# Sliding-window attention and a SwiGLU block: the first gate and value products begun with the head pairs that are ready, and q, k and v of later batches loaded earlier

## The chip, the core and the metric

One core of a Trainium2 chip runs the whole program. The time is device microseconds for one execution. Three runs of the kernel before took 276.92, 277.04 and 277.45 us.

## The reference

Attention over 4 batches, 8 heads, 768 positions and 64 columns per head, with 8 global keys and a window of 96, then a feed-forward block on the 3072 tokens of 512 columns.

```python
scores = scale * np.matmul(q, k.transpose(0, 1, 3, 2))
keep = is_global | is_local
bias = -slopes[:, None, None] * dist[None, :, :]
a = softmax(np.where(keep, scores + bias, -1e9))     # cut
x = (a @ v).transpose(0, 2, 1, 3).reshape(3072, 512)
g = x @ w_gate
silu = g * (1.0 / (1.0 + np.exp(-g)))
out = (silu * (x @ w_val)) @ w_out
```

## The kernel before, in words

The heads of a batch go in four pairs. A pair has four kinds of steps: `transposes` (q and k are turned on TensorE into `trq` and `trk`, and copied to `qT` and `kT`), `scores` (three banks `bk` 0 to 2 of key chunks; exp on ScalarE into `at`, then a product with the masks on VectorE or POOL, L234 and L238), and `values` for either half of the 768 queries (`den` and `num` on TensorE, two VectorE transposes and a reciprocal, and the product that writes `xT`; on VectorE in batch 0, L282, and on POOL later, L279). `xT` holds the attention's output with the columns of a head pair on the partitions, so that pair `hp` is contraction chunk `c = hp` of the products that follow.

The feed-forward block runs over 8 blocks `t` of 384 tokens. Each block has 12 groups `f` of 128 columns; for each, `gate_or_val` makes a gate product (`gps`) and a value product (`vps`) of four matmuls, one per chunk `c`, in one PSUM bank each. ScalarE makes `th` from the gate, VectorE `sl` from `th` and the gate (L313) and `hT` from `sl` and the value (L317). `out_part` (`ops`) turns `hT` of block `t - 1` into output rows, three matmuls at a time. The banks of the products go round by `state["x"]`: `x0`, `x1`, `x2`, `o0` in block 0 and the first three later, so that the third gate waits until VectorE has read the first.

Order is written out by hand, and each engine takes its instructions in that order. The prologue (L378 to L386) runs the four pairs of batch 0 for the first half, two stages apart. Then the list `groups` (gates, values, output parts) is walked, and the steps of the attention still to do (`plan`) are put between them: each group has a work number, a quota turns work into steps, and when a whole step is owed it is issued.

All loads are DMAs that POOL issues in its own queue, between its products; a DMA converts float32 to float16. Those of batch 0, the weights, and parts of batch 1 stand ahead of everything else (L342 to L362). The rest is issued at fixed places: `loads` (L424 to L431) maps 12 `t` + `f` to `load_qk` and `load_v_rest`. An issue waits until the load eight places ahead of it in the queue has landed.

Of the kernel before, what the change touches and what calls it, by code (L numbers as in the profile page):

```python
# [9 lines left out]
FP32 = mybir.dt.float32  # L10
# [27 lines left out]
def kernel(  # L38
# [18 lines left out]
    NP = H // 2  # L57
# [4 lines left out]
    NC = DM // 128  # L62
    J = S // 128
    NCH = 7
    TB = 384
# [18 lines left out]
    ps = ctx.enter_context(tc.tile_pool(name="ps", bufs=1, space=bass.MemoryType.PSUM))  # L84
# [21 lines left out]
    def stage(b):  # L106
        qst[b] = sb2.tile([128, H, J * D], FP16, name="qst", tag="qst")
        kst[b] = sb2.tile([128, H, J * D], FP16, name="kst", tag="kst")

    def load_qk(b, h0, h1):  # L110
        for st, src in ((qst[b], q), (kst[b], k)):
            nc.gpsimd.dma_start(  # L112
                out=st[:, h0:h1, :],
                in_=src[b, h0:h1].rearrange("h (p j) d -> p h (j d)", p=128))
# [6 lines left out]
    def load_v_rest(b, c):  # L121
        n = min(KC, S - KC * c)
        nc.gpsimd.dma_start(  # L123
            out=vSs[b][NG:NG + n, c, :, :],
            in_=v[b, :, KC * c:KC * c + n, :].rearrange("h p d -> p h d"))
# [18 lines left out]
    def load_w(g):  # L144
        f0 = WF * g
        for w, src in ((wg, moe_w_gate), (wv, moe_w_val)):
            nc.gpsimd.dma_start(
                out=w[:, :, f0:f0 + WF],
                in_=src[:, f0:f0 + WF].rearrange("(c p) f -> p c f", p=128))

    def load_wo(g):
        nc.gpsimd.dma_start(
            out=wo[:, 4 * g:4 * g + 4, :],
            in_=moe_w_out[512 * g:512 * g + 512].rearrange("(f p) d -> p f d", p=128))
# [4 lines left out]
    attn_tags = ["a0", "a1", "a2", "a3"]  # L159
    pro_tags = ["a0", "a1", "a2", "a3", "x0", "x1", "x2", "o0"]  # L160
    state = {"tags": pro_tags, "n": 0, "x": ["x0", "x1", "x2", "o0"]}
# [8 lines left out]
    def make_masks(h, c0, c1):  # L170
        nc.scalar.activation(
            out=masks[:, h, c0:c1], in_=dist[:, c0:c1], func=AF.Exp, scale=-slopes[h])
# [3 lines left out]
    def run_later(n):  # L176
        for _ in range(n):
            if later:
                later.pop(0)()
# [114 lines left out]

    gv = {}

    def gate_or_val(t, f, which):
        if f == 0 and which == 0:
            hTs[t] = sb2.tile([128, NFF, TB], FP16, name="hT", tag="hT")
        w = (wg, wv)[which]  # L300
        dst = ps.tile([128, 512], FP32, name="gv"[which] + "ps", tag=state["x"][gv.get("n", 0) % len(state["x"])])
        gv["n"] = gv.get("n", 0) + 1
        for c in range(NC):
            nc.tensor.matmul(  # L304
                dst[:, 0:TB], lhsT=w[:, c, 128 * f:128 * f + 128],
                rhs=xT[:, c, TB * t:TB * t + TB],
                start=(c == 0), stop=(c == NC - 1))

        if which == 0:
            th = sb2.tile([128, TB], FP32, name="th", tag="th")  # L310
            nc.scalar.activation(out=th, in_=dst[:, 0:TB], func=AF.Tanh, scale=0.5)  # L311
            sl = sb2.tile([128, TB], FP32, name="sl", tag="sl")
            nc.vector.scalar_tensor_tensor(  # L313
                out=sl, in0=th, scalar=1.0, in1=dst[:, 0:TB], op0=AluOp.add, op1=AluOp.mult)
            gv["sl"] = sl
        else:
            nc.vector.tensor_mul(hTs[t][:, f, :], dst[:, 0:TB], gv["sl"])  # L317
# [3 lines left out]
    def out_part(t, i, part):  # L321
        if part == 0:
            tag = ["a0", "a1", "o0"][i] if t == TOK // TB - 1 else "o0"
            ops_t[0] = ps.tile([128, 512], FP32, name="ops", tag=tag)
        ops = ops_t[0]
        for f in range(3 * part, 3 * part + 3):
            nc.tensor.matmul(  # L327
                ops, lhsT=hTs[t][:, f, 128 * i:128 * i + 128], rhs=wo[:, f, :],
                start=(f == 0), stop=(f == NFF - 1))
        if part == 3:  # L330
            osb = sb2.tile([128, DM], FP32, name="osb", tag="osb")
            nc.scalar.mul(out=osb, in_=ops, mul=0.5)  # L332
            r0 = TB * t + 128 * i
            nc.sync.dma_start(out=out[r0:r0 + 128, :], in_=osb)
# [17 lines left out]
    for c in range(4, NCH):  # L352
        load_v_rest(0, c)
    load_w(2)
    load_w(3)
    load_wo(0)
    load_qk(1, 0, 2)
    load_wo(1)
    load_wo(2)
    load_qk(1, 2, 4)  # L360
# [6 lines left out]
    def early(hp, s):  # L367
        p = pairs[0, hp]
        if s == 0:
            p.transposes()  # L370
        elif s < 3:
            p.scores(s - 1, nc.vector)
        else:
            p.values(0, True)

    make_masks(0, 0, BANK)
    make_masks(1, 0, BANK)
    for t in range(4 + 2 * (NP - 1)):  # L378
        for hp in range(NP):
            s = t - 2 * hp  # L380
            if 0 <= s < 4:
                early(hp, s)
                run_later(9)
                if s == 1 and hp + 1 < NP:
                    make_masks(2 * hp + 2, 0, BANK)
                    make_masks(2 * hp + 3, 0, BANK)  # L386
    for h in range(H):
        make_masks(h, BANK, 3 * WIN)
    state["tags"] = attn_tags
    state["n"] = 0  # L390


    def sc(b, hp, bk):
# [29 lines left out]

    loads = {10: [lambda: load_qk(1, 4, 8)]}  # L424
    for c in range(4, NCH):
        loads[14 + c] = [lambda c=c: load_v_rest(1, c)]
    for b, base, step in ((2, 23, 1), (3, 38, 2)):
        loads[base] = [lambda b=b: (stage(b), load_qk(b, 0, 4))]
        loads[base + step] = [lambda b=b: load_qk(b, 4, 8)]
        for c in range(NCH):  # L430
            loads[base + step * (2 + c)] = [lambda b=b, c=c: load_v_rest(b, c)]  # L431
# [3 lines left out]
    groups = []  # L435
    for t in range(NT):
        for f in range(NFF):
            groups.append((t, f, 1.0, lambda t=t, f=f: gate_or_val(t, f, 0)))
            groups.append((t, f, 1.0, lambda t=t, f=f: gate_or_val(t, f, 1)))
            if t > 0:  # L440
                groups.append((t, f, 1.1, lambda t=t, f=f: out_part(t - 1, f // 4, f % 4)))
    todo, quota = [], {}
# [67 lines left out]
```

## Time and profile before

| | |
|---|---|
| median of three runs | 277.04 us |
| the profiled execution | 276.11 us |
| its span, first to last instruction | 274.3 us |
| TensorE (PE) busy | 250.5 us, 91% |
| VectorE (DVE) busy | 179.6 us, 65% |
| ScalarE (ACT) busy | 141.4 us, 52% |
| POOL busy | 113.4 us, 41% |
| mean granted TensorE clock | 0.988 |

Times in the rows are microseconds from the start of the span. A row of the timeline gives the start, the duration, the engine, the line, what is written and read, how many instructions it joins and, in brackets, how long the engine stood idle ahead and who released it. A matmul's duration is from its start to its modelled end, so that matmuls in a row overlap. A granted clock of 1.00 is 2.4 GHz and 0.50 is 1.2 GHz. "PEld" is the loading of a matmul's weights.

### The profile page before, as it was taken

What the parts mean: (1) busy time and instruction counts of PE and PEld (TensorE: products, weight loads), DVE (VectorE), ACT (ScalarE), POOL (GpSimd) and SP (SyncE); (2) the same over time, 40 slices, a digit from 0 to 9 for tenths busy, and PEclk for the clock granted to TensorE, in tenths of its full rate; (3) what the DMA queues carried; (4) which work ended last, traced back from release to release, by engine and by line L of the source; (5) the groups of instructions that cost most, each with busy time, mean ns of one, the idle gap of its engine ahead of it and who ended that gap; (6) DMA issues with size and microseconds to landing.
All of it is one profiled execution on the core that took longest, in us unless ns stands there. A gap on an engine that the chain in (4) does not pass through costs nothing.

```text
span 274.3 us, 5703 instructions
## 1 busy us (share of the span) xinstructions
PE 250.5 (91%) x2240; PEld 143.3 (52%) x2240; DVE 179.6 (65%) x389; ACT 141.4 (52%) x297; POOL 113.4 (41%) x130
## 2 busy tenths in 40 slices
PE   1786988899999599998999999999999999999994
PEld 0563355555556364655556555565556555555541
DVE  2588697878778539576674778576787855555520
ACT  3678445486656365766456646665473333323321
POOL 8965535164358906741756517344171400000000
PEclk9998699999999999999999999999999999999999
DMA  8999999900170993701598153201101000001011
GB/s 104 171 169 191 200 204 197 170 8 0 42 81 2 178 148 56 83 2 41 76 204 82 45 33 58 46 2 39 41 0 41 38 38 24 18 38 41 38 76 76
DMA packets 45529, 21.27 MB, mean 78 GB/s; under 512 B 28256, under 2 KB 42432, under 8 KB 45504
## 3 DMA queue, kind: packets, MB, share of 16 engines
q0 software_dynamic: 41504, 14.20, 45.7%
q1 hardware_dynamic: 4000, 6.72, 6.7%
q8 instruction: 17, 0.28, 0.4%
q14 instruction: 8, 0.07, 0.1%
HBM read 28.58 MB, written 6.29 MB: 127 GB/s over the span
## 4 chain that ended last, share of the span: by engine, by line
PE 70%; DMA 13%; DVE 5%; POOL 5%; ACT 3%; issue 2%; DVEq 0%; ACTq 0%; POOLq 0%
PE ops L327 21%; PE vps L304 19%; PE gps L304 19%; DMA kst<-in_k_dram 9%; DMA wv<-in_moe_w_val_dram 4%; PE den L256 3%; PE scA L221 3%; PE num L256 2%; POOL qst L112 1%; POOL vS L117 1%; PE trk L193 1%; DVE rb L275 1%; DVE sl L313 1%; DVE dT L269 1%; DVE hT L317 1%
## 5 line engine op out<-in xcount | busy, mean ns | idle before, releaser
L311 ACT ACTIVATE th<-gps 128x384 f32<-128x384 f32 x96 | 47.8, 498 | 70.2 <-PE gps L304 67.8
L313 DVE SCALAR_TENSOR_TENSOR sl<-th,gps 128x384 f32<-128x384 f32 x96 | 52.3, 545 | 44.7 <-ACT th L311 44.6
L304 PE MATMUL gps<-xT,wg 128*128 128x384 f16 x384 | 79.7, 330 | 0.8 <-DVE xT L282 0.6
L304 PE MATMUL vps<-xT,wv 128*128 128x384 f16 x384 | 78.9, 328 | 1.2 <-DVE sl L313 1.1
L327 PE MATMUL ops<-wo,hT 128*128 128x512 f16 x288 | 76.0, 380 | 0.0
L317 DVE TENSOR_TENSOR hT<-vps,sl 128x384 f16<-128x384 f32 x96 | 52.5, 547 | 8.4 <-PE vps L304 1.8
L279 POOL TENSOR_TENSOR xT<-ns,rb 128x384 f16<-128x384 f32 x24 | 24.0, 1001 | 72.0 <-DVE rb L275 63.7
L304 PEld LDWEIGHTS <-wg 128*128 128x128 f16 x384 | 36.3, 99 | 32.8 <-issue 2.0
L304 PEld LDWEIGHTS <-wv 128*128 128x128 f16 x384 | 36.3, 98 | 26.7 <-issue 3.6
L327 PEld LDWEIGHTS <-hT 128*128 128x128 f16 x288 | 27.1, 98 | 24.8 <-issue 0.7
L227 ACT ACTIVATE at<-scA 128x432 f16<-128x432 f32 x48 | 25.8, 537 | 13.4 <-PE scB L221 13.4
L234 POOL TENSOR_TENSOR at<-at,masks 128x432 f16<-128x432 f16 x24 | 24.8, 1053 | 13.5 <-ACT at L227 13.2
L238 DVE TENSOR_TENSOR at<-at,masks 128x432 f16<-128x432 f16 x52 | 26.7, 540 | 1.3 <-ACT at L227 1.2
L227 ACT ACTIVATE at<-scB 128x432 f16<-128x432 f32 x48 | 26.1, 544 | 0.0
L332 ACT ACTIVATE osb<-ops 128x512 f32<-128x512 f32 x24 | 14.3, 597 | 19.7 <-PE ops L327 19.7
L123 POOL DMA_DIRECT2D vS<-in_v_dram x24 | 21.5, 900 | 4.0 <-issue 2.0
L256 PE MATMUL den<-at,ones 128*64 128x216 f16 (+6 forms) x288 | 18.0, 240 | 2.9 <-DVE at L238 1.8
L290 ACT COPY ns<-num 128x384 f32<-128x384 f32 x24 | 11.5, 478 | 15.9 <-PE num L256 14.0
L275 DVE STREAM_TRANSPOSE rb<-dR 128x384 f32<-128x384 f32 x32 | 18.3, 572 | 1.0
L256 PEld LDWEIGHTS <-ones 128*64 128x64 f16 x288 | 12.1, 114 | 13.0 <-issue 10.3
L269 DVE STREAM_TRANSPOSE dT<-den 128x384 f32<-128x384 f32 x32 | 18.2, 570 | 0.4 <-PE den L256 0.4
L193 PE MATMUL trq<-ident,qst 128*64 128x128 f16 x192 | 9.5, 244 | 8.8 <-DMA qst<-in_q_dram 8.1
(32 smaller groups left out, 189.7 us busy)
## 6 DMA issues: line engine op xcount, KB each, us to landing
out_dram<-osb SPq DMA_DIRECT2D x24, 256.0 KB, 2.0
vS<-in_v_dram POOLq DMA_DIRECT2D x20, 120.0 KB, 4.1
qst<-in_q_dram POOLq DMA_DIRECT2D x5, 384.0 KB, 8.2
kst<-in_k_dram POOLq DMA_DIRECT2D x5, 384.0 KB, 8.9
wg<-in_moe_w_gate_dram POOLq DMA_DIRECT2D x4, 384.0 KB, 10.3
wv<-in_moe_w_val_dram POOLq DMA_DIRECT2D x4, 384.0 KB, 11.2
wo<-in_moe_w_out_dram POOLq DMA_DIRECT2D x3, 512.0 KB, 14.2
qst<-in_q_dram POOLq DMA_DIRECT2D x6, 192.0 KB, 6.6
```

Source lines behind the costliest of these rows:

```text
L123: nc.gpsimd.dma_start(out=vSs[b][NG:NG + n, c, :, :], in_=v[b, :, KC * c:KC * c + n, :].rearrange("h p d -> p h d"))
L227: nc.scalar.activation(out=at, in_=sc[hi][:, 0:BANK], func=AF.Exp, scale=scale)
L234: mul_eng.tensor_mul(a2, a2, m[:, WIN:2 * WIN].unsqueeze(1).broadcast_to([128, 2, WIN]))
L238: mul_eng.tensor_mul(at, at, m[:, o:o + BANK])
L256: nc.tensor.matmul(dst[r, o:o + n], lhsT=ones if ones_side else vSs[b][:, c, 2 * hp + hi, :], rhs=self.at[hi, cb][:, col:col + n], start=( ...
L275: nc.vector.transpose(rb[:, 0:n_q].rearrange("p (n i) -> p n i", i=32), dR[:, 0:nb].unsqueeze(2).broadcast_to([128, nb, 32]))
L279: nc.gpsimd.tensor_mul(dst, ns[:, 0:n_q], rb[:, 0:n_q])
L304: nc.tensor.matmul(dst[:, 0:TB], lhsT=w[:, c, 128 * f:128 * f + 128], rhs=xT[:, c, TB * t:TB * t + TB], start=(c == 0), stop=(c == NC - 1))
L311: nc.scalar.activation(out=th, in_=dst[:, 0:TB], func=AF.Tanh, scale=0.5)
L313: nc.vector.scalar_tensor_tensor(out=sl, in0=th, scalar=1.0, in1=dst[:, 0:TB], op0=AluOp.add, op1=AluOp.mult)
L317: nc.vector.tensor_mul(hTs[t][:, f, :], dst[:, 0:TB], gv["sl"])
L327: nc.tensor.matmul(ops, lhsT=hTs[t][:, f, 128 * i:128 * i + 128], rhs=wo[:, f, :], start=(f == 0), stop=(f == NFF - 1))
```

## The change

`gate_or_val` is split: `products` issues the matmuls for chunks `c0` to `c1`, and the rest of it finishes the group. Of the first four groups of block 0 (gate and value for f = 0 and f = 1), chunks 0 and 1 of the f = 0 pair are issued between the last scores of the prologue and the values of the last pair; after those values come chunk 2 of the f = 0 pair and chunks 0 to 2 of the f = 1 pair; the last chunk is issued where the group stood. Their work number goes from 1.0 to 0.25. The banks of the last two prologue steps are chosen so that `x0` and `x1` are free. Of the loads, q and k for the first pair of batch 1 go from behind the first `wo` to ahead of the last gate and value weights; the last v chunks of batch 1 go from 12 t + f = 18 to 20 to 12 to 14; q, k and v of batch 2 begin at 15 in place of 23, and those of batch 3 at 32 in place of 38.

```diff
-    def gate_or_val(t, f, which):
-        if f == 0 and which == 0:
+    def products(t, f, which, c0, c1):
+        if f == 0 and which == 0 and c0 == 0:
             hTs[t] = sb2.tile([128, NFF, TB], FP16, name="hT", tag="hT")
+        if c0 == 0:
+            gv[f, which] = ps.tile(
+                [128, 512], FP32, name="gv"[which] + "ps",
+                tag=state["x"][gv.get("n", 0) % len(state["x"])])
+            gv["n"] = gv.get("n", 0) + 1
         w = (wg, wv)[which]
-        for c in range(NC):
+        for c in range(c0, c1):
             nc.tensor.matmul(
-                dst[:, 0:TB], lhsT=w[:, c, 128 * f:128 * f + 128],
+                gv[f, which][:, 0:TB], lhsT=w[:, c, 128 * f:128 * f + 128],
                 rhs=xT[:, c, TB * t:TB * t + TB],
                 start=(c == 0), stop=(c == NC - 1))
+
+    def gate_or_val(t, f, which, c0=0):
+        products(t, f, which, c0, NC)
+        dst = gv.pop((f, which))
...
     load_w(2)
+    load_qk(1, 0, 2)
     load_w(3)
     load_wo(0)
-    load_qk(1, 0, 2)
     load_wo(1)
...
+    head = [(0, 0), (0, 1), (1, 0), (1, 1)]
     for t in range(4 + 2 * (NP - 1)):
+        if t == 7:
+            state["tags"] = attn_tags + ["x2", "o0"]
+            state["n"] = 0
         for hp in range(NP):
             s = t - 2 * hp
             if 0 <= s < 4:
+                if hp == NP - 1 and s == 3:
+                    for f, which in head[:2]:
+                        products(0, f, which, 0, 2)
                 early(hp, s)
...
+    state["tags"] = attn_tags
+    state["n"] = 2
+    for f, which in head:
+        products(0, f, which, 0 if f else 2, NC - 1)
     for h in range(H):
         make_masks(h, BANK, 3 * WIN)
-    state["tags"] = attn_tags
-    state["n"] = 0
...
-        loads[14 + c] = [lambda c=c: load_v_rest(1, c)]
-    for b, base, step in ((2, 23, 1), (3, 38, 2)):
+        loads[8 + c] = [lambda c=c: load_v_rest(1, c)]
+    for b, base, step in ((2, 15, 1), (3, 32, 2)):
...
+            begun = t == 0 and f < 2
+            c0 = NC - 1 if begun else 0
+            groups.append((t, f, 0.25 if begun else 1.0,
+                           lambda t=t, f=f, c0=c0: gate_or_val(t, f, 0, c0)))
```

On TensorE, at the end of the prologue (the scores of the last pair, `kT_79`, and its values, which begin with `den`; the piece of the difference):

```order
 L221 MATMUL scB<-qT,kT_79 128x216
+L307 LDWEIGHTS wg
+L307 MATMUL gps<-xT,wg 128x384
+L307 LDWEIGHTS wv
+L307 MATMUL vps<-xT,wv 128x384
 L256 LDWEIGHTS ones
 L256 MATMUL den<-at,ones 64x216
```

Each of the two products stands there with two matmuls, where the values followed the scores at once.

In POOL's queue, in the prologue (the loads from the third gate weights to the second q and k of batch 1; the piece of the difference):

```order
 L147 DMA wg<-in_moe_w_gate_dram 128x4x384
 L147 DMA wv<-in_moe_w_val_dram 128x4x384
+L112 DMA qst<-in_q_dram 128x2x384
+L112 DMA kst<-in_k_dram 128x2x384
 L147 DMA wg<-in_moe_w_gate_dram 128x4x384
 L147 DMA wv<-in_moe_w_val_dram 128x4x384
-L152 DMA wo<-in_moe_w_out_dram 128x4x512
-L112 DMA qst<-in_q_dram 128x2x384
-L112 DMA kst<-in_k_dram 128x2x384
-L152 DMA wo<-in_moe_w_out_dram 128x4x512 x2
+L152 DMA wo<-in_moe_w_out_dram 128x4x512 x3
 L112 DMA qst<-in_q_dram 128x2x384
```

The q and k of batch 1's first pair move ahead of two weight loads and one `wo`; those of its second pair, the last row, stay behind the same loads.

In POOL's queue in block 1, in the changed kernel (`vS_85` is v of batch 1, `vS_86` of batch 2, and the q and k are those of batch 2):

```order
L123 DMA vS_85<-in_v_dram 120x8x64
L279 TENSOR_TENSOR xT<-ns,rb 128x384
L123 DMA vS_85<-in_v_dram 120x8x64
L234 TENSOR_TENSOR at<-at,masks 128x432 x2
L123 DMA vS_85<-in_v_dram 48x8x64
L112 DMA qst<-in_q_dram 128x4x384
L112 DMA kst<-in_k_dram 128x4x384
L279 TENSOR_TENSOR xT<-ns,rb 128x384
L112 DMA qst<-in_q_dram 128x4x384
L112 DMA kst<-in_k_dram 128x4x384
L234 TENSOR_TENSOR at<-at,masks 128x432 x2
L123 DMA vS_86<-in_v_dram 120x8x64 x2
```

In the kernel before, no load stands between these products, and the four q and k of batch 2 come only behind the last mask products of batch 1.

## Rows read from the trace of the kernel before

**Rows 1.** Busy time by stretch: stretch, length, busy (instructions) per engine, clock, DMA share, GB/s.

```profile
24.00:25.60 1.60, 0.00 (x1) 0.00 (x1) 1.48 (x4) 1.60 (x5) 0.66 (x1) 0.97 1.39 194
25.60:32.40 6.80, 6.17 (x34) 2.83 (x34) 4.61 (x11) 3.46 (x11) 3.71 (x6) 0.51 1.61 190
51.30:57.30 6.00, 4.95 (x58) 2.76 (x58) 5.01 (x13) 4.12 (x11) 0.69 (x1) 1.00 0.73 108
...
57.27:92.00 34.73, 34.73 (x340) 20.10 (x339) 28.21 (x58) 22.21 (x49) 22.27 (x24) 1.00 0.26 35
...
92.10:95.70 3.60, 0.60 (x15) 0.43 (x16) 0.93 (x2) 1.29 (x2) 3.60 (x4) 1.00 1.25 221
...
96.00:262.00 166.00, 164.31 (x1390) 93.65 (x1386) 109.52 (x226) 84.21 (x176) 54.81 (x57) 1.00 0.32 51
```

**Rows 2.** Chain that ended last, one gate of block 0: start, length, engine, line.

```profile
44.15 0.65 PE gps L304 x4
```

**Rows 3.** Timeline, the first gates of block 0 and the first sl.

```profile
27.24 1.14 PE L304 MATMUL gps<-xT,wg 128*128 128x384 f16 x3
...
28.99 0.48 PE L304 MATMUL gps<-xT,wg 128*128 128x384 f16 x1 [0.61 <-DVE xT L282]
...
30.03 0.55 DVE L313 SCALAR_TENSOR_TENSOR sl<-th,gps 128x384 f32<-128x384 f32 x1 [1.09 <-ACT th L311]
...
33.43 0.81 PE L304 MATMUL gps<-xT,wg 128*128 128x384 f16 x4
```

**Rows 4.** Timeline, transposes on TensorE: batch 1's pairs, then the first of batch 2.

```profile
41.89 0.53 PE L193 MATMUL trq<-ident,qst 128*64 128x128 f16 x12 [1.36 <-DMA qst<-in_q_dram]
...
42.87 0.53 PE L193 MATMUL trk<-ident,kst 128*64 128x128 f16 x12 [0.46 <-DMA kst<-in_k_dram]
...
52.14 0.53 PE L193 MATMUL trq<-ident,qst 128*64 128x128 f16 x12 [0.71 <-DVE xT L282]
...
52.47 0.53 PE L193 MATMUL trk<-ident,kst 128*64 128x128 f16 x12
...
60.29 0.50 PE L193 MATMUL trk<-ident,kst 128*64 128x128 f16 x12
...
92.94 0.53 PE L193 MATMUL trq<-ident,qst 128*64 128x128 f16 x12 [0.83 <-DMA qst<-in_q_dram]
...
95.64 0.53 PE L193 MATMUL trk<-ident,kst 128*64 128x128 f16 x12 [2.17 <-DMA kst<-in_k_dram]
```

**Rows 5.** Waits of TensorE: engine, line, released by: us in total, times, longest.

```profile
PE trk L193 <- DMA kst<-in_k_dram: 3.0, 3, 2.2
```

**Rows 6.** Timeline of POOL: issues of wv, batch 1's second and third k, batch 2's k.

```profile
16.02 0.77 POOL L147 DMA_DIRECT2D wv<-in_moe_w_val_dram  x1 [1.07 <-DMA kst<-in_k_dram]
...
36.66 0.70 POOL L112 DMA_DIRECT2D kst<-in_k_dram  x1 [1.24 <-DMA wg<-in_moe_w_gate_dram]
...
48.20 0.76 POOL L112 DMA_DIRECT2D kst<-in_k_dram  x1 [1.79 <-DMA wo<-in_moe_w_out_dram]
...
88.83 0.76 POOL L112 DMA_DIRECT2D kst<-in_k_dram  x1
```

**Rows 7.** DMA issues of those four moments: KB each, us to landing.

```profile
wv<-in_moe_w_val_dram POOLq DMA_DIRECT2D x1, 384.0 KB, 8.6
...
kst<-in_k_dram POOLq DMA_DIRECT2D x1, 192.0 KB, 13.2
...
kst<-in_k_dram POOLq DMA_DIRECT2D x1, 384.0 KB, 8.9
...
kst<-in_k_dram POOLq DMA_DIRECT2D x1, 384.0 KB, 6.8
```

**Rows 8.** The page: GB/s moved in 40 slices of 6.86 us.

```profile
GB/s 104 171 169 191 200 204 197 170 8 0 42 81 2 178 148 56 83 2 41 76 204 82 45 33 58 46 2 39 41 0 41 38 38 24 18 38 41 38 76 76
```

**Rows 9.** Timeline, batch 1's last mask product on POOL and the values that read it.

```profile
73.70 2.25 POOL L234 TENSOR_TENSOR at<-at,masks 128x432 f16<-128x432 f16 x2
...
78.02 0.45 PE L256 MATMUL den<-at,ones 128*64 128x216 f16 x8
```

More of the change, by code (lines that the diff above doesn't have):

```diff
@@ L295 @@
     gv = {}
-    def gate_or_val(t, f, which):
-        if f == 0 and which == 0:
+    def products(t, f, which, c0, c1):
+        if f == 0 and which == 0 and c0 == 0:
             hTs[t] = sb2.tile([128, NFF, TB], FP16, name="hT", tag="hT")
+        if c0 == 0:
[3 more added lines that the diff above has]
+            gv["n"] = gv.get("n", 0) + 1
         w = (wg, wv)[which]
-        dst = ps.tile([128, 512], FP32, name="gv"[which] + "ps", tag=state["x"][gv.get("n", 0) % len(state["x"])])
-        gv["n"] = gv.get("n", 0) + 1
-        for c in range(NC):
+        for c in range(c0, c1):
             nc.tensor.matmul(
-                dst[:, 0:TB], lhsT=w[:, c, 128 * f:128 * f + 128],
+                gv[f, which][:, 0:TB], lhsT=w[:, c, 128 * f:128 * f + 128],
                 rhs=xT[:, c, TB * t:TB * t + TB],
                 start=(c == 0), stop=(c == NC - 1))
+    def gate_or_val(t, f, which, c0=0):
+        products(t, f, which, c0, NC)
+        dst = gv.pop((f, which))
         if which == 0:
@@ L437 @@
         for f in range(NFF):
-            groups.append((t, f, 1.0, lambda t=t, f=f: gate_or_val(t, f, 0)))
-            groups.append((t, f, 1.0, lambda t=t, f=f: gate_or_val(t, f, 1)))
+            begun = t == 0 and f < 2
+            c0 = NC - 1 if begun else 0
+            groups.append((t, f, 0.25 if begun else 1.0,
+                           lambda t=t, f=f, c0=c0: gate_or_val(t, f, 0, c0)))
+            groups.append((t, f, 0.25 if begun else 1.0,
+                           lambda t=t, f=f, c0=c0: gate_or_val(t, f, 1, c0)))
             if t > 0:
```

## The prediction

> **What bounds the kernel now.** I read the waits of TensorE first, then the timeline of the two stretches that the diff touches, then the issues and landings of the loads, and the busy times by stretch last. From 57 to 92 us TensorE is busy 34.73 of 34.73 us, and from 96 to 262 us 164.31 of 166.00 [rows 1]; four gate or value matmuls take 0.65 us at full clock [rows 2]. So time can only be taken out where TensorE stands still or runs at half clock. Three such places lie in the reach of the change.
> The first is the end of the prologue. TensorE does nothing from 24.0 to 25.6 us, and the granted clock then goes from 1.00 to 0.50, that is from 2.4 to 1.2 GHz, until 32.4 us [rows 1]: 6.17 us of busy time at half rate, about 3.1 us lost, and 0.61 us of waiting for the last head pair's xT within it [rows 3]. The second is the transposes of batch 1, which wait 1.36 and 0.46 us for q and k [rows 4]. The third is the transposes of batch 2, 0.83 and 2.17 us, 3.0 us in sum, all of it DMA [rows 4]; the waits by kind agree, as their longest for k is the 2.2 us there [rows 5].
> Landings follow from two rows each, the start of the issue on POOL [rows 6] plus the time to landing [rows 7]; both groups stand in the order wv, batch 1's k of heads 2 and 3, its k of heads 4 to 7, batch 2's first k. The check is batch 2's first k: 88.83 + 6.8 = 95.6, and its transposes start at 95.64 [rows 4].
>
> **The change part by part.** No instruction is added or removed; 4,482 rows stand on TensorE before and after. What moves:
> *Head of block 0.* Four of the sixteen matmuls go between the last scores and the last pair's values, eight behind the values, and the four final terms behind xT. The first four need the first weights of wg and wv; wv lands at 16.02 + 8.6 = 24.6 [rows 6, 7], a microsecond before the values start at 25.6, so they cost nothing and lie in the idle 1.6 us. The eight lie between the values and 28.99, when xT comes [rows 3]. At full clock they take 1.3 us of the 1.75 us after 27.24; at half clock 2.6 us, and overrun it by 0.8.
> The final gate term then starts at 28.99. Today its sl starts 1.04 us later and takes 0.55 [rows 3]; at full clock the matmul's record is some 0.15 us shorter, so the bank of the first gate is free at 28.99 + 0.89 + 0.55 = 30.4, and the third gate, which takes that bank, starts there instead of at 33.43. One set of scores, 0.3 us, is then still to do that was done before. Gain at this point: 33.43 - 30.4 - 0.3 = 2.7 us. If the clock falls as before, the gate ends 0.8 us later and some of what follows is at half rate: 1.2 us.
> *What is late next.* From the third gate to the second transposes of batch 1 took 52.14 - 33.43 = 18.7 us, with waits of 1.36, 0.46 and 0.71 in it [rows 4]; without them 16.2. In the new order the first q and k of batch 1 stand two weight loads sooner in POOL's queue. The set of q, k, weights 3 and the first wo is the same, and all of it had landed by 42.87 before, so the weights of f = 9 are there in time, as their gate comes last ahead of these transposes. The first transposes lose their wait. TensorE then reaches the second ones at 30.4 + 0.3 + 16.2 = 46.9.
> But the q and k of those heads still stand behind the same bytes. k was issued at 36.66 and landed 13.2 later, at 49.9, q about 1.0 sooner (the two waits of the first transposes end 1.0 apart) [rows 4, 6, 7]. The queue has been moving around 200 GB/s without a gap from 27 to 48 us (slices 5 to 7 of 40) [rows 8], so a new order inside it leaves 49.9 where it is. **A new wait of about 2 us for q and 0.6 us for k takes the place of the old ones.** The k transposes start at 49.9 in place of 52.47: 2.6 us gained, whatever the head gave beyond that.
> The same happens once more: the last k of batch 1 lands at 48.20 + 8.9 = 57.1, and today its transposes start at 60.29 [rows 4, 6, 7]. In the new order one output piece of three matmuls (0.65) stands behind them instead of ahead, so the gain there is at most 60.29 - 0.65 - 57.1 = 2.5 us. Between the two places TensorE needs 60.29 - 52.47 - 0.65 = 7.2 us, of which 0.3 was waiting (1.05 idle from 51.3 to 57.3 [rows 1], less the 0.71 that lies ahead of 52.14): from 49.9 it gets to 56.8, inside the 57.1. Without a fall of the clock: **2.5 us**.
> *The clock in the new wait.* Two rows bracket it. From 24.0 to 25.6 us TensorE stood still for 1.6 us and the clock fell; from 92.1 to 95.7 us it was busy only 0.60 of 3.60 us and the clock stayed at 1.00 [rows 1]. The new wait, 2.6 us with one set of transposes in it, is like the second in shape and like the first in its longest piece. A fall costs between nothing and what the one spell in the trace cost, 3.1 us. After the wait TensorE has dense work and no later wait, so I take half, 1.5 us, for a fall: 56.8 + 1.5 = 58.3, a gain of 59.64 - 58.3 = 1.3 us. The two bracketing rows are equally near, so between 2.5 and 1.3 I take 2.0.
> The Trainium skill, page TensorE: Matmul & The Clock Gate, section on HAM oscillation, speaks against the head change here: a TensorE that outruns its loads is throttled in the wait and begins the next piece cold, so speed won ahead of a wait is paid back behind it. The fall after 24.0 to 25.6 agrees and 92.1 to 95.7 does not; by the page alone the first part would be worth nearly nothing, the first rival below.
> *Loads of batch 2.* Eight groups of f sooner, q and k are issued near 70 us and need 6.8 us for the first k here [rows 7]; their transposes come near 90. The 3.0 us go whole: both waits end with a landing and with nothing else [rows 4]. POOL takes the cost: four q/k issues and seven for v, 0.7 to 1.0 us each, now stand among its mask products and xT products of batch 1. Nearest is the mask product of the last pair, 73.70 to 75.95, needed at 78.02 [rows 9]: 2.1 us to spare, of which two q/k issues behind the xT product take 1.5. Free by 0.6.
> *Loads of batch 3, and v of batch 1.* The first had no wait and get none; the v chunks are needed at 87 us and go sooner. Nothing.
> *Step order.* Steps of later blocks come about one group later against the products. The waits that depend on this, after 96 us, come to 166.00 - 164.31 = 1.7 us in the trace [rows 1]; I take nothing, and 0.7 either way for the range.
> **Sum:** 2.0 + 3.0 = 5.0 us. The profiled execution took 276.11 us (span 274.3), 0.93 under the median of the three runs, 277.04; it would come to 271.1, and the median to **272.0 us**.
>
> **The rivals.**
> (1) *The clock falls in the new wait and stays down as long as before*, 6.8 us. For it: the fall at 25.6 came after less idle time. Against: the work behind is denser. Gain 2.5 + 0.3 - 3.1 = -0.3, and 3.0 from batch 2: 274.3. Chance 0.20. The rule of the Trainium skill's page TensorE: Matmul & The Clock Gate makes this case.
> (2) *POOL becomes late.* If its issues cost more than the 0.6 us left, the values of the last pair wait for the mask product, and with them the xT of the next block. Two such waits of the size of a product, 1 us each: 274.0. For it: POOL has nearly no gap left from 66 to 90 us. Against: loads go as soon as POOL reaches them, before the products are ready. Chance 0.09.
> (3) *The queue is not the limit*, and loads come sooner with the new order. Then no new wait appears: 2.7 + 1.36 + 0.46 + 0.71 + 3.0 = 8.2, 268.8 us. Against it are the even 200 GB/s. Chance 0.04. The Trainium skill's page DMA: Bandwidth & Descriptors, section Specifications, gives a ceiling of 435 GB/s for the fabric, by which this would hold; the rows show less than half, and I go by them.
> (4) *Slower.* TensorE comes out of the new wait at half clock, is held up again at 57.1 for the last k, and does not get back to the full clock until batch 1 is through. Place: 50 to 65 us. Every microsecond at half clock costs half of one, so with the 0.3 us of room ahead of 57.1 a spell of over 11.6 us eats the whole 5.5; 15 us, an estimate from the length of that stretch, costs 7.5, a loss of 1.7: 278.7 us. Against it: the one spell under dense work lasted 6.8. Chance 0.05.
> That the order isn't what the diff says can be left out, as the queues show it.
>
> **How the numbers follow.** The forecast has 0.62: 271.2 to 273.0 by itself (2.5 or 1.3 in the first part, 0.3 for steps). To hold 8 in 10 the range takes in most of (1) and (2) above and goes below to the full 2.5 with 0.7 from the steps (277.04 - 6.2 = 270.8) and a little under, as runs differ: **270.6 to 274.5**. Two runs of this kernel can be told apart by about 0.2%, 0.55 us. The cases other than (4) are all faster by over 2 us; I leave 0.02 for two losses at once that end near zero. Faster 0.92, same 0.02, slower 0.06.
>
> **What would show it.** Right: the transposes of the first heads of batch 1 without a wait; a wait for q near 47 to 49 and for k until about 50 at the second heads; the last k's transposes at 57 to 58; none in batch 2; the third gate near 30.4. The granted clock from 50 to 57 decides between the forecast and (1) and (4). Wrong: if the wait at 50 us is missing, (3); if a wait for mask products stands near 75 us, (2); if the clock falls at 25.6 as before, the head's 2.7 was 1.2, but the landing at 49.9 hides most of the difference.

## The result and the profile after

The changed kernel takes 270.59 us (median of four runs, 270.38 to 271.07) against 277.03 us before: ratio 0.9767, 95% interval 0.9749 to 0.9785. The forecast was 272.0 us with a range from 270.6, so the time lies 0.01 us outside it, on the fast side. The profiled execution took 270.38 us.

The page of the changed kernel, against [rows 8] and the table ahead of the prediction:

```profile
span 268.5 us, 5705 instructions
...
PE 247.8 (92%) x2240; PEld 142.2 (53%) x2240; DVE 181.3 (68%) x389; ACT 141.0 (53%) x297; POOL 113.0 (42%) x130
...
PEclk9999999999999999999999999999999999999999
...
GB/s 105 167 170 193 195 205 205 177 46 37 212 166 45 44 39 2 157 103 92 57 60 37 49 1 42 39 4 39 42 38 4 39 43 39 7 32 42 39 78 78
```

The span is 5.8 us shorter. The clock row has no dip left, and the queue still moves about 200 GB/s over the same slices.

Timeline of TensorE in the changed kernel, the head and the third gate (against [rows 3]), the transposes of batch 1's first three pairs and of batch 2's first (against [rows 4]):

```profile
23.75 0.50 PE L307 MATMUL gps<-xT,wg 128*128 128x384 f16 x2
...
28.91 0.32 PE L307 MATMUL gps<-xT,wg 128*128 128x384 f16 x1 [0.53 <-DVE xT L282]
...
30.40 0.81 PE L307 MATMUL gps<-xT,wg 128*128 128x384 f16 x4 [0.28 <-DVE sl L320]
...
39.66 0.53 PE L193 MATMUL trq<-ident,qst 128*64 128x128 f16 x12
40.02 0.50 PE L193 MATMUL trk<-ident,kst 128*64 128x128 f16 x12
...
48.35 0.53 PE L193 MATMUL trq<-ident,qst 128*64 128x128 f16 x12 [0.71 <-DVE xT L282]
48.69 0.53 PE L193 MATMUL trk<-ident,kst 128*64 128x128 f16 x12
...
56.45 0.50 PE L193 MATMUL trk<-ident,kst 128*64 128x128 f16 x12
...
88.16 0.50 PE L193 MATMUL trk<-ident,kst 128*64 128x128 f16 x12
```

The final gate term takes 0.32 us, the full-clock duration, where it took 0.48. The third gate starts at 30.40, as the prediction had it. No transposes of batches 1 to 3 wait for a DMA any more: not the first pair, not batch 2, and not the second pair either, where the prediction had its new wait. Those wait 0.71 us for VectorE's xT, as they did before.

The longest of the new waits was not in the prediction (same timeline):

```profile
137.64 0.81 PE L307 MATMUL gps<-xT,wg 128*128 128x384 f16 x4 [1.30 <-DVE hT L324]
```

**Where the 5.8 us of the span came from.** I cut both traces at rows that do the same work: the k transposes of batch 1's last pair (68.17 before, 63.68 after) and those of batch 2's third pair (115.11 and 107.11). The rows, first before, then after:

```profile
68.17 0.50 PE L193 MATMUL trk<-ident,kst 128*64 128x128 f16 x12
...
115.11 0.50 PE L193 MATMUL trk<-ident,kst 128*64 128x128 f16 x12
```

```profile
63.68 0.50 PE L193 MATMUL trk<-ident,kst 128*64 128x128 f16 x12
...
107.11 0.50 PE L193 MATMUL trk<-ident,kst 128*64 128x128 f16 x12
```

At both places the changed kernel has 1.3 us of products still to do that stood ahead before, since it comes to its steps sooner: at the first cut four gate or value matmuls (0.65) and an output piece of three (0.65), at the second eight gate or value matmuls. Up to the first cut: 68.17 - (63.68 + 1.3) = 3.2 us gained. Between the cuts: 46.94 against 43.43, 3.5 gained. From the second cut to the end: 159.2 against 161.4 - 1.3 = 160.1, 0.9 lost. The sum, 5.8, is the whole difference. It is that of one execution each; the second set has more, and the parts move.

### The profile page after: what moved, and what is told of

The parts are those of the page before. It is cut to its first block, busy times and chain, and to the rows that moved or that the text cites. A ratio compares the mean times of both kernels' runs of the same rounds, so it can differ in the third digit from the quotient of the medians.

```text
span 268.5 us, 5705 instructions
## 1 busy us (share of the span) xinstructions
PE 247.8 (92%) x2240; PEld 142.2 (53%) x2240; DVE 181.3 (68%) x389; ACT 141.0 (53%) x297; POOL 113.0 (42%) x130
## 3 DMA queue, kind: packets, MB, share of 16 engines
q0 software_dynamic: 41504, 14.20, 46.6%
HBM read 28.58 MB, written 6.29 MB: 130 GB/s over the span
## 4 chain that ended last, share of the span: by engine, by line
PE 74%; DVE 14%; ACT 7%; issue 2%; DMA 2%; POOL 0%; DVEq 0%; ACTq 0%; POOLq 0%
PE ops L334 22%; PE vps L307 20%; PE gps L307 19%; PE den L256 4%; PE scA L221 3%; ACT at L227 3%; PE num L256 3%; DVE sl L320 3%; DVE at L238 2%; DVE hT L324 2%; DMA kst<-in_k_dram 2%; DVE kT L204 1%; DVE rb L275 1%; DVE dT L269 1%; DVE xT L282 1%
## 5 line engine op out<-in xcount | busy, mean ns | idle before, releaser
L307 PE MATMUL gps<-xT,wg 128*128 128x384 f16 x384 | 78.8, 326 | 2.1 <-DVE hT L324 1.3
L227 ACT ACTIVATE at<-scA 128x432 f16<-128x432 f32 x48 | 25.8, 537 | 16.2 <-PE scB L221 16.2
L238 DVE TENSOR_TENSOR at<-at,masks 128x432 f16<-128x432 f16 x52 | 28.1, 566 | 2.1 <-ACT at L227 1.7
L221 PE MATMUL scA<-qT,kT 64*128 64x216 f16 (+2 forms) x112 | 15.0, 255 | 3.2 <-DVE kT L208 2.4
```

The lines of the kernel that those rows point to most:

```text
L221: nc.tensor.matmul(sc[hi][:, col:col + n], lhsT=self.kT[r, 128 * c:128 * c + 128], rhs=self.qT[r, q0:q0 + n], start=True, stop=True)
L227: nc.scalar.activation(out=at, in_=sc[hi][:, 0:BANK], func=AF.Exp, scale=scale)
L238: mul_eng.tensor_mul(at, at, m[:, o:o + BANK])
L307: nc.tensor.matmul(gv[f, which][:, 0:TB], lhsT=w[:, c, 128 * f:128 * f + 128], rhs=xT[:, c, TB * t:TB * t + TB], start=(c == 0), stop=(c = ...
```

## The experiments

### The change taken apart

Four kernels that ran beside each other; the kernel before took 277.19 us there (274.60 to 278.29).

**The new head with the old loads** (edit against the changed kernel):

```diff
-    load_qk(1, 0, 2)
     load_w(3)
     load_wo(0)
+    load_qk(1, 0, 2)
...
-        loads[8 + c] = [lambda c=c: load_v_rest(1, c)]
-    for b, base, step in ((2, 15, 1), (3, 32, 2)):
+        loads[14 + c] = [lambda c=c: load_v_rest(1, c)]
+    for b, base, step in ((2, 23, 1), (3, 38, 2)):
```

> The new head with every load in its old place. Theory A (the head and the earlier q and k of batch 1 only work together): TensorE reaches the first transposes of batch 1 near 39.7 us as in the changed kernel, but their q and k still land near 41.8 and 42.8, so it waits about 3 us and is only 1.3 us (one gate and one value more done) ahead of the kernel before at that point; batch 2 still waits 3.0 us. Time about 275.5 us, or up to 277 if the clock falls in the wait. Rival B (the head is worth the 3.2 us measured at batch 1's third transposes by itself): about 273.8 us.

Measured: 275.31 us, ratio 0.994 (0.9903 to 0.9976). Theory A has the time, though the first transposes of batch 1 waited 0.96 and 0.45 us and not about 3, as q and k were there a microsecond sooner than in the profile of before. TensorE comes to batch 2 sooner and stands there all the same (0.77 and 1.86 us), and behind the wait the clock falls (by windows; columns as in [rows 1]):

```profile
92.00:94.00 2.00, 1.65 (x38) 1.30 (x39) 0.29 (x1) 1.08 (x3) 2.00 (x3) 0.89 0.97 137
94.00:96.00 2.00, 2.00 (x8) 0.93 (x7) 0.64 (x3) 1.64 (x4) 1.01 (x2) 0.50 1.22 176
```

That half-clock spell is not in the profile of before, which had a slightly longer wait there (0.83 and 2.17).

**The new loads with the old head**, that is, only the load lines of the change:

```diff
     load_w(2)
+    load_qk(1, 0, 2)
...
-        loads[14 + c] = [lambda c=c: load_v_rest(1, c)]
-    for b, base, step in ((2, 23, 1), (3, 38, 2)):
+        loads[8 + c] = [lambda c=c: load_v_rest(1, c)]
+    for b, base, step in ((2, 15, 1), (3, 32, 2)):
```

> Every load in its new place, the head as before. Theory A: the waits of 1.36, 0.46, 0.83 and 2.17 us go, the fall of the clock from 25.6 to 32.4 us stays: 277.0 - 4.8 = 272.2 us. Rival B (the loads are worth batch 2's 3.0 us alone, as the head takes the rest): 274.0 us.

Measured: 270.75 us, ratio 0.9768 (0.9726 to 0.9809), level with the whole change and below both theories. The half-clock spell at 25.6 is still there, and no transposes of batches 1 to 3 wait for a DMA.

**Of the loads only v of batch 1 and batches 2 and 3**, with the old head and batch 1's q and k where they were:

```diff
-        loads[14 + c] = [lambda c=c: load_v_rest(1, c)]
-    for b, base, step in ((2, 23, 1), (3, 38, 2)):
+        loads[8 + c] = [lambda c=c: load_v_rest(1, c)]
+    for b, base, step in ((2, 15, 1), (3, 32, 2)):
```

> Only the v loads of batch 1 and the q, k and v loads of batches 2 and 3 sooner; the q and k of batch 1's first pair and the head as before. Theory A: 3.0 us less, 274.0 us, with no wait at batch 2's transposes and the waits of 1.36 and 0.46 us left. Rival (POOL's issues among its products give part of it back): over 275 us, with waits for mask products near 75 us.

Measured: 272.25 us, ratio 0.9828 (0.978 to 0.9876): 4.9 us, more than the 3.0 us of waits that these loads remove in the trace of before, so both theories missed. In its profile the first transposes of batch 1 have no wait for a DMA either: TensorE came to them only at 41.59.

**The changed kernel with work number 1.0**, so that the steps of the attention keep the places that they had:

```diff
-            groups.append((t, f, 0.25 if begun else 1.0,
+            groups.append((t, f, 1.0,
```

> The changed kernel with the work number of the four begun groups back at 1.0, so that the steps of the attention stand between the same groups as in the kernel before. If the about 1 us that the changed kernel loses again after 96 us comes from the shifted steps: about 269.6 us, and the wait of 1.30 us near 137.6 us is gone. Rival (those waits come wherever the steps stand, or the third set of scores now comes too late): within 0.5 us of the changed kernel, 270.6.

Measured: 269.49 us, ratio 0.9733 (0.9678 to 0.9788), about 1.1 us better than the change, and the wait near 137.6 us is gone, as was expected. So the smaller work number takes something back; where, the third set shows.

### The same code again

These four ran on another chip, where the kernel before took 275.38 us (274.48 to 278.19): the changed kernel, the one with work number 1.0, and the kernel before twice, for its profile alone.

> The changed kernel once more, beside the next one on the same chip. Theory A (the new head saves about 1.2 us on top of the loads, and the smaller work number costs as much again): 270.6 us, and 1.2 us more than with the work number back at 1.0. Rival (the difference of the two was that of the runs, which spread by more than 2 us): the same time within 0.5 us.

> The changed kernel with the work number 1.0, beside the changed kernel on the same chip. Theory A: 269.5 us, the waits after 96 us as in the kernel before (1.7 us). Rival: 270.5 us.

> The kernel before once more, for its profile. Theory A (in most executions the wait of batch 2 also lets the clock fall, which the first profile did not show; that is why sooner loads for batch 2 gained 4.9 us and not 3.0): a span of about 276 us with a spell of granted clock 0.50 behind 93 us. Rival (the clock falls at 25 us alone, and the times differ by how long that spell lasts): the spell there is longer than 6.8 us and none behind 93 us.

> The kernel before a third time, for its profile: the same two theories; with Theory A most of the profiles with a span over 275 us show a spell of 0.50 behind 93 us.

The changed kernel took 270.89 us (ratio 0.9811, 0.9767 to 0.9856), the one with work number 1.0 269.46 (0.9757, 0.9716 to 0.9798), the two executions of before 276.07 and 277.35. So the smaller work number costs 1.4 us on one chip, and Theory A holds for the first two runs. In both executions of before the clock falls in the wait of batch 2, as Theory A has it there. The transposes there in the first (timeline), the stretch around them (windows), and the transposes in the second (timeline):

```profile
94.24 0.85 PE L193 MATMUL trk<-ident,kst 128*64 128x128 f16 x12 [1.87 <-DMA kst<-in_k_dram]
```

```profile
93.00:97.00 4.00, 2.76 (x39) 2.26 (x40) 0.18 (x1) 2.08 (x5) 1.70 (x2) 0.60 1.26 230
```

```profile
95.29 0.67 PE L193 MATMUL trk<-ident,kst 128*64 128x128 f16 x12 [2.14 <-DMA kst<-in_k_dram]
95.75 0.85 PE L193 MATMUL trq<-ident,qst 128*64 128x128 f16 x12
```

The transposes take 0.85 us where [rows 4] have 0.53. The stretch between the two cuts took 46.94 us in the profile of before, 47.97 and 48.55 in these, and 43.68 in each of the kernels with the new loads and the old places of the steps. Without the wait of batch 2 this stretch is 3.3 us shorter when the clock held in the wait, and 4.3 and 4.9 when it fell.

The part ahead of the first cut moves as well. In both executions the first transposes of batch 1 waited 0.43 us for k alone, where [rows 4] have 1.36 and 0.46, and the cut came sooner than at 68.17 (timeline, first one, then the other):

```profile
41.80 0.53 PE L193 MATMUL trk<-ident,kst 128*64 128x128 f16 x12 [0.43 <-DMA kst<-in_k_dram]
...
67.10 0.50 PE L193 MATMUL trk<-ident,kst 128*64 128x128 f16 x12
```

```profile
42.51 0.53 PE L193 MATMUL trk<-ident,kst 128*64 128x128 f16 x12 [0.43 <-DMA kst<-in_k_dram]
...
67.81 0.50 PE L193 MATMUL trk<-ident,kst 128*64 128x128 f16 x12
```

So the first of them took 276.07 us, as the profiled execution of the prediction did (276.11), with a fall at batch 2 that the other did not have.

The other wait, which the prediction put at batch 1's second pair, stands in the profile of the kernel with work number 1.0 on that chip:

```profile
49.41 0.53 PE L193 MATMUL trq<-ident,qst 128*64 128x128 f16 x12 [1.32 <-DMA qst<-in_q_dram]
50.44 0.53 PE L193 MATMUL trk<-ident,kst 128*64 128x128 f16 x12 [0.50 <-DMA kst<-in_k_dram]
50.89 0.82 PE L307 MATMUL gps<-xT,wg 128*128 128x384 f16 x4
```

The end of that wait is within 0.6 us of the 49.9 that was forecast, and the four gate matmuls behind it take 0.82 us: here the clock did not fall. On the chip of the first set the same code had 0.16 us of it, since k was there at 49.0. A landing that depends on the whole queue ahead of it moves by more than a microsecond from execution to execution.

### Three single questions, and one run again

These ran together; the kernel before took 277.08 us there (275.21 to 278.23).

**What does a wait at batch 1's second pair cost?** Its q and k go behind four v loads:

```diff
-    load_qk(1, 2, 4)
     for c in range(4):
         load_v_rest(1, c)
+    load_qk(1, 2, 4)
```

> The changed kernel with one thing moved: q and k of batch 1's heads 2 and 3 are issued behind the four v loads of batch 1 in place of ahead of them, so 480 KB more stand ahead of them; at 200 GB/s (an estimate from the rows of GB/s) they land 2.4 us later, q near 49.9 and k near 50.9. TensorE comes to their transposes at 47.6 to 48.4. (A) A wait costs its length and no more: q's wait is 1.5 to 2.3 us, k's 0.5, the k transposes of the third pair come at about 58.7 in place of 56.45, and the time is 270.6 + 2.2 = 272.8 us, range 272.3 to 273.3. (B) The wait also takes the clock down, as the prediction half expected: a stretch at 0.50 behind it, another 1 to 3 us, 273.8 to 275.8. (C) VectorE sets the pace of block 0, so that most of the wait is made good by the third pair: under 271.4.

Measured: 274.82 us (274.14 to 275.98), ratio 0.9917 (0.9883 to 0.9951), 4.2 us above the changed kernel. (B) holds by the time. Timeline of TensorE:

```profile
51.41 0.53 PE L193 MATMUL trq<-ident,qst 128*64 128x128 f16 x12 [3.77 <-DMA qst<-in_q_dram]
52.41 0.53 PE L193 MATMUL trk<-ident,kst 128*64 128x128 f16 x12 [0.47 <-DMA kst<-in_k_dram]
52.87 1.46 PE L307 MATMUL gps<-xT,wg 128*128 128x384 f16 x4
...
56.33 0.82 PE L307 MATMUL gps<-xT,wg 128*128 128x384 f16 x4
...
61.21 0.50 PE L193 MATMUL trk<-ident,kst 128*64 128x128 f16 x12
```

Four gate matmuls take 1.46 us behind the wait and 0.82 again from 56.33: a spell at half clock. The k transposes come 52.41 - 48.69 = 3.72 us later than in the changed kernel, and the next pair's 61.21 - 56.45 = 4.76 later. The wait costs its length, the clock 1.0 us on top, and nothing is made good. The wait was longer than expected, as q landed at 51.4 and not at 49.9: the estimate for its size was poor.

**Where does the wait at 137.64 come from?** Batch 3's loads go back:

```diff
-    for b, base, step in ((2, 15, 1), (3, 32, 2)):
+    for b, base, step in ((2, 15, 1), (3, 38, 2)):
```

> The changed kernel with q, k and v of batch 3 issued where they were before (from place 38 in place of 32). The wait of 1.30 us for hT at 137.64, which the kernel before does not have, costs most of the 0.95 us by which the stretch behind batch 2 is longer than before. (A) It comes from batch 3's loads, which now stand among POOL's products of batch 2: the wait goes, 270.6 - 0.95 = 269.7 us. (B) It comes from the order of steps that the work number 0.25 makes: it stays, 270.6 us, within 0.4.

Measured: 269.37 us (268.98 to 269.75), ratio 0.9719 (0.9678 to 0.9759), level with the 269.46 to 269.49 of the kernel with work number 1.0. (A) holds: the wait is gone. From the second cut to the end this kernel takes 267.5 - 107.66 = 159.8 us against 161.4, with its steps at the same places. The rows that differ, first of the changed kernel: timeline of VectorE and POOL, then the two mask products of line L238 by themselves (durations min/median/max in ns):

```profile
133.20 3.92 DVE L238 TENSOR_TENSOR at<-at,masks 128x432 f16<-128x432 f16 x2
...
133.93 0.96 POOL L123 DMA_DIRECT2D vS<-in_v_dram  x1
134.90 1.97 POOL L238 TENSOR_TENSOR at<-at,masks 128x432 f16<-128x432 f16 x2
```

```profile
L238 DVE TENSOR_TENSOR at<-at,masks x2: 1019/2000/2980, 133.2 to 134.1; 128x432 f16<-128x432 f16 x2
```

and the same two views of the one with batch 3's loads back:

```profile
133.74 2.12 DVE L238 TENSOR_TENSOR at<-at,masks 128x432 f16<-128x432 f16 x2
...
134.47 0.99 POOL L123 DMA_DIRECT2D vS<-in_v_dram  x1
135.49 2.20 POOL L238 TENSOR_TENSOR at<-at,masks 128x432 f16<-128x432 f16 x2
```

```profile
L238 DVE TENSOR_TENSOR at<-at,masks x2: 1021/1101/1181, 133.7 to 134.7; 128x432 f16<-128x432 f16 x2
```

In the changed kernel VectorE's second mask product takes 2.98 us and ends at 137.12, just behind POOL's two products. hT stands behind it, and TensorE behind hT. In the other kernel the same product takes 1.18 and ends at 135.86, and it is POOL's pair that is longer, 2.20 against 1.97. That the load moved the wait is shown; that the two engines exclude each other, and that a few hundredths of a microsecond decide which goes first, is how I read the rows, and no run tests it. With work number 1.0 and the same loads TensorE has no such wait, so the two edits collide only together.

**Does VectorE set the pace of block 0?** Work number 1.0, and the second-half xT products of batch 0 on POOL:

```diff
-        return lambda: pairs[b, hp].values(half, b == 0)
+        return lambda: pairs[b, hp].values(half, b == 0 and half == 0)
...
-    loads = {10: [lambda: load_qk(1, 4, 8)]}
+    loads = {0: [lambda: load_qk(1, 4, 8)]}
```

(The buffers `rb` and `ns` are four deep there.)

> The changed kernel with work number 1.0 for the first four groups (269.5 us so far) and the second-half xT products of batch 0 moved from VectorE to POOL, as later batches have them. (A) VectorE's xT, hT and sl are what holds TensorE in block 0 (about 1.1 us of waits for xT and den's at): these waits shrink, and the time is 268.7 us, range 268.2 to 269.2, if the landing of q and k at 48.5 to 50.4 leaves room; where it doesn't, a wait for q takes their place and the time stays near 269.5. (B) POOL, which issues the loads at that time and takes longer for such a product, becomes late: values or transposes wait for xT or for loads issued later, 270 to 271.5 us.

Measured: 270.77 us (270.24 to 270.91), ratio 0.9765 (0.9732 to 0.9799). Timeline of TensorE:

```profile
37.83 0.50 PE L193 MATMUL trk<-ident,kst 128*64 128x128 f16 x12
...
48.00 0.53 PE L193 MATMUL trq<-ident,qst 128*64 128x128 f16 x12 [1.64 <-DMA qst<-in_q_dram]
49.04 0.53 PE L193 MATMUL trk<-ident,kst 128*64 128x128 f16 x12 [0.51 <-DMA kst<-in_k_dram]
49.50 0.82 PE L307 MATMUL gps<-xT,wg 128*128 128x384 f16 x4
...
56.27 0.81 PE L334 MATMUL ops<-wo,hT 128*128 128x512 f16 x3 [1.37 <-DVE hT L324]
```

The time is in (B)'s range, but both theories had half of it. The first k transposes come at 37.83 against 39.08 with work number 1.0 alone, so VectorE's xT did hold TensorE up to there; behind them it waits for q, and lands where it was. Then VectorE's hT is 1.37 us late, beside mask products on POOL, and the time is worse than with xT on VectorE. This run also issues the third pair's q and k sooner; that share is not told apart.

**The new loads with the old head, again,** the edit as in the first set:

> The kernel before with all loads of the change and the head as it was, a second time and beside the others. (A) The split head is worth about 1.2 us where the steps keep their places: 270.7 us, 1.0 to 1.4 over the version of it with work number 1.0. (B) That difference was the chips': within 0.5 us of the others.

Measured: 271.12 us (270.58 to 271.54), ratio 0.978 (0.9745 to 0.9816). Against the kernel with batch 3's loads back, which has the new head and no collision, that is 271.12 - 269.37 = 1.75 us; against the one with work number 1.0 it was 270.75 - 269.49 = 1.26 in the first set. So the head is worth 1.3 to 1.8 us where nothing takes it back. (B) is out; (A) holds but for its size, as 1.75 lies over its 1.0 to 1.4.

## Why the prediction was right in sign and short in size

**The head.** Right at its place: 30.40 predicted and measured, with the clock held. In the second profile of the changed kernel two gate matmuls took 0.82 us at 24.21, half clock, where the first has 0.50, and the third gate still started at 30.51. But of the 2.7 us only 40.35 - 39.08 = 1.3 us are left at batch 1's first k transposes (old head against new, both with the new loads and the old places of the steps; on a second pair of runs 40.90 - 39.55, the same). TensorE has new waits for xT, 0.65 us ahead of these transposes and 0.32 behind them in the changed kernel, as VectorE's chain of xT, sl and hT is no faster than before. It came to the second transposes at 47.64 in place of the 46.9 forecast, and stood there 0.71 us for xT, as before. The sum had taken that wait out of its 16.2 us without a reason, and had left out who is late next on VectorE. The half-clock spell of [rows 1], counted as 3.1 us lost, was mostly hidden by that chain, as I read these rows.

**The first part, taken as 2.0, was 3.2 in one pair of profiles and 2.5 on average.** The first cut came at 68.17, 67.10 and 67.81 us in the three profiles of before, and at 63.68, 63.81 and 64.22 in the three that have the changed kernel's code up to there (the change twice, and the one with batch 3's loads back). With the 1.3 us still to do that is a gain of 1.6 to 3.2 us, 2.5 between the means: what the sum had without a fall of the clock. That the size came out so near is in part luck, since the new wait, its reason, did not come in either profile of the changed kernel. q of the second pair landed at 33.34 + 14.2 = 47.5 and k at 34.29 + 14.2 = 48.5 (issues and landings of the changed kernel), 1.4 before the forecast, and TensorE arrived later than forecast, so that the new wait closed from both sides. That such a wait can come, the second chip and the run with late q and k show; the landing was forecast as one number where it is a spread of 2 us. The half-priced fall of the clock did not happen, as there was no wait to cause it. So rival (1) did not come about, and what rival (3) said of the wait came true without its reason: the queue is no faster. Its 200 GB/s are bytes as written in float16: by the page the loads' queue wrote 14.20 MB and 28.58 MB were read from HBM, so about 400 GB/s were read (an estimate from these numbers). "Less than half" in rival (3) compared the written bytes alone.

The rule on oscillation from the Trainium skill's page TensorE: Matmul & The Clock Gate, by which speed won ahead of a wait is paid back behind it, held in the run with late q and k (1.46 us for four gate matmuls behind the wait). It did not hold behind the shorter waits of 1.32 and 0.50 us and of 1.64 and 0.51 us, where four gate matmuls took 0.82. It did not apply to the changed kernel, which has no such wait.

**Batch 2, taken as 3.0, is the step that failed.** "The 3.0 us go whole" counted the two waits of one execution and nothing behind them. Moving the loads takes away 3.3 us in that execution, and 4.3 and 4.9 in the two others of the same kernel, in which the wait also dropped the clock: 4.1 on average. On these averages it is, of the terms that came out larger than forecast, the furthest off; on the first pair of profiles alone the first part is (3.2 against 2.0). Three executions are few. The prediction priced a fall for the wait that it expected to add, and none for the wait that it removed, because the one trace showed none there. The same mistake sits in the last line of the sum: the profiled execution's 0.93 us under the median was carried over, as if it were a constant. After the change the gap is 270.59 - 270.38 = 0.21. Profile against profile, the forecast was 271.1 and the result 270.38; the other half of the miss is that offset. That the fall at batch 2 makes up the offset is not shown, since runs without a profile don't tell their stretches; the profile of before that took 276.07 us had the fall and made it good with a shorter first part.

**Batch 3, taken as nothing, cost 1.2 to 1.6** (270.59 against 269.37 us; 161.4 against 159.8 behind the second cut). "The first had no wait and get none" looked at landings alone. Its issues on POOL moved a mask product so that VectorE's hT came late: near rival (2) in that POOL's issues cost time, but through VectorE, and 60 us behind the place that it named. POOL did keep gaps there: it was busy 18.74 of 24 us from 66 to 90 us in the changed kernel, its issues counted. The room of 2.1 us in [rows 9] was kept, as no wait stands near 75 us.

**Step order, taken as 0 with 0.7 either way.** Without the collision, the new places of the steps end the stretch behind the second cut at 159.8 - 1.3 = 158.5 us against 159.2: a gain of 0.7, inside what was allowed. Against it stands that collision, which only these places meet. The times show less of a gain: 269.37 us without the collision, and 269.46 to 269.49 with the old places.

The terms as measured on the first pair of profiles are 3.2 + 3.5 - 0.9 = 5.8, against 5.0 predicted. On the averages over three profiles of before they are 2.5 + 4.4 - 0.9 = 6.0, where 4.4 is the stretch between the cuts with the new places of the steps (47.8 against 43.4); the medians differ by 6.4. The prediction counts 4,482 rows on TensorE; the page has 2240 matmuls and 2240 weight loads in either kernel, and nothing rests on the difference.

## What to carry to other kernels

A wait for a DMA costs its length and, in some executions, a clock that has fallen behind it; price that for waits that an edit removes as for those that it adds, from more than one profile, and don't carry a profile's distance from the median through the edit. What a faster TensorE wins is checked against the next engine in the chain before it is counted. A load on POOL's queue that comes earlier than anyone needs it is not free: here the change without its earlier batch 3, or with work number 1.0, takes 269.4 to 269.5 us in place of 270.6.

## What was not expected of the hardware

- One VectorE product took 2.98 us beside POOL's products, with a median of 0.38 over all 52 of its line. The Trainium skill's page SBUF — State Buffer, section SBUF: two separate sides, says that a VectorE operation with two SBUF inputs and a GpSimd operation that reads SBUF take turns on one port pair, held for a whole instruction, the other blocked. The rows agree: the product ended 0.25 us behind POOL's second product. It was held from 134.1 us on, while POOL issued a DMA and then through two products in a row. The issue alone does not explain this: with work number 1.0 two such products took 0.38 us each (134.22 to 134.89) while POOL issued a DMA from 134.29 to 135.25. What decides is open.
- The same wait dropped the clock in two of three profiled executions of one kernel (transposes of 0.85 us behind it in place of 0.53).
- The granted clock of a profile can miss a spell. In the second run of the new loads with the old head it reads 1.00 (window; columns as in [rows 1]), while three gate matmuls take 1.14 us (timeline), as at 0.51 in [rows 1, 3]:

```profile
25.40:32.40 7.00, 6.23 (x34) 2.83 (x34) 4.76 (x12) 3.79 (x12) 4.32 (x6) 1.00 1.62 188
```

```profile
27.19 1.14 PE L304 MATMUL gps<-xT,wg 128*128 128x384 f16 x3
```

Where the two differ, durations decide.
